# Block-sparse attention and a mixture of experts on one core: three wide token units instead of two, a small tile behind each, and hand order to the last jump

## The chip, the core and the metric

The kernel runs on one core of one Trainium2 chip. A core has five engines that run side by side: TensorE (PE in the profile; its weight loads are PEld), VectorE (DVE), ScalarE (ACT), GpSimd (POOL) and SyncE (SP), and 16 DMA engines that move data between the device's memory and the on-chip memory. Each engine works through its own queue of instructions in order and waits on semaphores for the others. The metric is the device time of one execution in microseconds, the median of several runs.

## The reference

Two blocks stand one behind the other. Attention has 4 batches, 8 heads, 768 tokens and head size 64; a query block of 32 tokens sees its neighbours, the first and last block, and three sampled blocks. Its output is laid out as 3072 rows of 512, and these rows go to eight experts, each row to the one with the largest logit:

```python
logits = x @ w_gate
expert_idx = np.argmax(logits, axis=1)
...
for e in range(E):
    lo, hi = (boundaries[e], boundaries[e + 1])
    ...
    h = np.maximum(x_sorted[lo:hi] @ w1[e], 0.0)
    y_sorted[lo:hi] = h @ w2[e]
y = y_sorted[inv_perm]
return (gate_w[:, None] * y).astype(np.float32)
```

Everything is float32. One expert has two matrices, w1 of 512 x 1024 and w2 of 1024 x 512, 2 MB each. How many rows an expert gets is known only at run time.

## The kernel before

**Attention** goes over 16 pairs of heads, four for each batch. For each pair and half of the queries it computes scores, their exponentials, the weighted values and the division, and writes rows of x to a scratch tensor in memory (`x_rows`). It fills the first half of the time and is not touched by the change.

**Routing** runs beside it. `ranks`, `count` and `layout_a` (phase A) place what is known after three batches: the first KA = 5 tiles of 128 rows, all of one expert each. Phase B (`layout_b`, lines 568 to 653) places the rest after the last batch. It turns counts into four kinds of work on VectorE, with vectors of eight numbers, one per expert:

- a *tile*: 128 rows of one expert (`turn_x`, `layer1`, `layer2`);
- a *unit*: more than 128 rows of one expert in one go, so that a remainder does not need a tile of its own (`gather_u`, `turn_u`, `layers_u`, `leave_u`). In layer 1 and layer 2 the weights stand still and the rows stream past, `width` of them, and four transposes per 128 rows put the result back into rows. The width is one of a few, chosen at run time by a `Switch` on `kind` (line 1036);
- a *small tile*: at most 32 rows of one expert, four column groups of TensorE at once (`gather_s`, `turn_s`, `layer1_s`, `turn_h`, `layer2_s`, `leave_s`);
- *tiles that may not come*: the program has NS tile places in its main loop. If routing needs more, a last `Switch` on `arm` (line 1067) runs 1, 2, ... further tiles; arm 0 runs none. `judge` (line 375) computes the arm, and also sends the whole kernel to a careful second pass if a check on the sums fails.

An expert's remainder behind its last full tile becomes part of a unit if it is at most QR rows and the expert has a tile to join it with; remainders of at most QS = 32 rows that stand alone become small tiles. NS (line 58) is the number of tile places that the worst allowed split needs once the units and small tiles are taken out.

**The main loop** (lines 996 to 1064) is a pipeline written out in program order. In step i it gathers the rows of tile i+3 (an indirect DMA that GpSimd issues), computes layer 1 of tile i+1, between its two halves turns the rows of tile i+2 (16 transposes of 32 x 32 blocks on VectorE), and computes layer 2 of tile i, which ScalarE scales by the gate weight and GpSimd scatters to `out`. Before step AT[u] unit u stands between layer 2 of tile AT[u]-1 and layer 2 of tile AT[u]. In step AT_S[k] small tile k is woven into layer 1 of tile i+1. A unit's rows are gathered in step AT[u]-3 and turned in step AT[u]-2.

**Weights** are fetched by SyncE, 2 MB at a time, into two buffers for w1 and two for w2, in the order of `in_order` (line 737): `fetch_after(what, layer)` fetches what stands two places behind `what`, since that one's buffer has just come free. A fetch waits for the last matmul that read the buffer. SyncE issues in its own queue's order.

**Who sets the order.** `tc.manual_schedule` (the stack `by_hand`) keeps TensorE, VectorE and GpSimd in program order. It is closed after step KA+1 = 6; from there on a scheduler orders all engines. ScalarE and SyncE are ordered by the scheduler throughout.

**On-chip memory.** Units and small tiles use slices of `ea`, the attention's large buffer: `hT_u`, `zT_u`, `xT_u`, `xg_u`, `zo_u` and, behind them, `xg_s`, `xT_s`, `hT_s`.

Of the kernel before, what the change touches and what calls it, by code (L numbers as in the profile page):

```python
# [7 lines left out]
F32 = mybir.dt.float32  # L8
BF16 = mybir.dt.bfloat16
I32 = mybir.dt.int32  # L10
AX = mybir.AxisListType.X
AF = mybir.ActivationFunctionType
ALU = mybir.AluOpType
# [4 lines left out]
def kernel(  # L18
# [11 lines left out]
    nc = tc.nc  # L30
    P = 128
# [7 lines left out]
    N, DM = out.shape  # L39
    E = moe_w_gate.shape[1]  # L40
    F = moe_w1.shape[2]
    DB = DM // P
    FB = F // P
# [2 lines left out]
    TA = NT - NCH  # L46
    KA = 5

    QR = P // 2
    MW = P + QR  # L50
    AT = (10, 13)
    KU = len(AT)

    QS = P // 4
    AT_S = (10, 13, 17)
    KS = len(AT_S)
    NS = KA - -(N - KA * P - KU * MW - KS * QS) // P
    NTB = NC - KA
    NB_ = NTB + 2 * KU + KS
    assert KA < AT[0] - 4 and AT[0] + 3 <= AT[1] < NS - 3 and AT_S[:KU] == AT and AT_S[-1] < NS - 3  # L60
    assert TA * P - E * (P - 1) > (KA - 1) * P
    XW = DM + 8
    scale = 1.0 / float(D) ** 0.5
# [131 lines left out]
    by_hand = ExitStack()  # L195
# [5 lines left out]
    sm = ctx.enter_context(tc.tile_pool(name="sm", bufs=1))  # L201
# [23 lines left out]
    rt = {}  # L225
# [268 lines left out]
    def small_e(name):  # L494
        return sm.tile([P, E], F32, name=name)
# [72 lines left out]
    def layout_b():  # L568
# [9 lines left out]
        nt, up, last = small_e("ntB"), small_e("upB"), small_e("last")  # L578
# [25 lines left out]
        w, ws, to = small_e("w"), small_e("ws"), small_e("to")  # L604
# [18 lines left out]
        )  # L623
        rt["more"] = more_f

        kind = small_e("kind")
        nc.vector.tensor_single_scalar(kind[:], last[:], QR / 2.0, op=ALU.is_gt)
        nc.vector.scalar_tensor_tensor(kind[:], in0=kind[:], scalar=1.0, in1=u[:], op0=ALU.add, op1=ALU.mult)

        xf = sm.tile([1, 2 * KU + KS], F32, name="xfU")  # L630
        for j, (number, n_, what) in enumerate(((at, KU, rt["eid"]), (at, KU, kind), (ws, KS, rt["eid"]))):
# [3 lines left out]
                op=ALU.is_equal,  # L635
# [94 lines left out]
    def gather(i):  # L730
        xg = st[i]["xg"] = keep_xg[i % 4]
        nc.gpsimd.indirect_dma_start(  # L732
            out=xg[:], out_offset=None, in_=x_d[: N - S, :] if i < KA else x_d[:, :], in_offset=bass.IndirectOffsetOnAxis(ap=of("g", i, P), axis=0),
        )
# [34 lines left out]
    def fetch_after(what, layer):  # L769

        fetch_at(orders[layer].index(what) + 2, layer)
# [49 lines left out]
    def layer2(i, group):  # L821
        zp = upper["ps_z"].tile([P, DM], F32, name="zp")
        layer2_pe(i, zp)
        zo = xp.tile([P, DM], F32, name="zo")
        weigh(i, zo, zp)
        put(of("s", i, P), zo[:], group)
# [9 lines left out]


    flat = ea.rearrange("p a b -> p (a b)")
    sizes = (FB * MW, DB * MW, DB * MW, 2 * XW, 2 * DM)
    parts = [flat[:, sum(sizes[:j]) : sum(sizes[: j + 1])] for j in range(len(sizes))]  # L840
    rest = flat[:, sum(sizes) :]
    hT_u = parts[0].rearrange("p (f t) -> p f t", f=FB)
    zT_u, xT_u = (p_.rearrange("p (c t) -> p c t", c=DB) for p_ in parts[1:3])
    xg_u, zo_u = (p_.rearrange("p (j w) -> p j w", j=2) for p_ in parts[3:])

    xg_s, xT_s, hT_s = (rest[:, a:b] for a, b in ((0, XW), (XW, XW + P), (XW + P, XW + 3 * P)))
    h_s, zo_s = parts[0][:, : 2 * P], parts[0][:, 2 * P : 3 * P]
    out_s = out.rearrange("n (g d) -> (n g) d", g=4)
    assert DB == 4 and F == 4 * 2 * P

# [40 lines left out]
    def leave_s(k_, group):  # L891
        put(rt["sS"][:, k_ : k_ + 1], zo_s, group, out_s)
# [102 lines left out]
    index = {}  # L995
    for i in range(NS):
        if i == 0:
            ranks("B", TA, NT)
        gather(i + 3)
        here = AT_S.index(i) if i in AT_S else None  # L1000
        if here is not None:
            layer1_s(here)
            fetch_after(("small", here), 1)
        if i + 1 < NS:
            layer1(i + 1, lambda: turn_x(i + 2), *([turn_h] if here is not None else []))
            if i + 3 <= NS:
                fetch_after(i + 1, 1)
        if here is not None:
            layer2_s(here)
            fetch_after(("small", here), 2)  # L1010
            leave_s(here, "rows_out")
        if i == 0:
            count("B")
            layout_b()
        if i + 3 in AT:
            gather_u(AT.index(i + 3))
        if i + 3 in AT_S:
            gather_s(AT_S.index(i + 3))
        if i + 2 in AT:
            turn_u()  # L1020
        if i + 2 in AT_S:
            turn_s()
        if i in AT:

            continue
        if i + 1 in AT:


            u = AT.index(i + 1)
            zps = [upper["ps_z"].tile([P, DM], F32, name="zp") for _ in range(2)]  # L1030
            zos = [xp.tile([P, DM], F32, name="zo") for _ in range(2)]
            banks = [upper["ps_h"].tile([P, DM], F32, name="hpu", tag="hp") for _ in range(2)]
            banks += [upper["ps_m"].tile([P, DM], F32, name="tpu", tag="tpg") for _ in range(2)] + zps[1:]
            layer2_pe(i, zps[0])
            fetch_after(i, 2)
            for more in tc.Switch(index[u], 3):
                weigh(i, zos[0], zps[0])
                layers_u(u, P + more * QR // 2, banks)
                layer2_pe(i + 1, banks[1])
                weigh(i + 1, zos[1], banks[1])  # L1040
            fetch_after(("unit", u), 1)
            fetch_after(("unit", u), 2)
            fetch_after(i + 1, 2)
            put(of("s", i, P), zos[0][:], "rows_out")
            leave_u(u, "rows_out")
            put(of("s", i + 1, P), zos[1][:], "rows_out")
            continue
        layer2(i, "rows_out")
        if i + 2 <= NS:
            fetch_after(i, 2)  # L1050
        if i == 1:
            tokens("B", NT, NB_)
        if i == 2:
            judge()
            tokens_s()
        if i == 3:
            for u in range(KU):
                at = rt["xeU"][0:1, KU + u : KU + u + 1]
                index[u] = {
                    mybir.EngineType.PE: nc.tensor.value_load(at, min_val=0, max_val=2),  # L1060
                    mybir.EngineType.Activation: nc.scalar.value_load(at, min_val=0, max_val=2),
                }
        if i == KA + 1:
            by_hand.close()
    lent.close()

    for arm in tc.Switch(nc.values_load(rt["arm"][0:1, 0:1], min_val=0, max_val=REDO), REDO + 1):
        inside = ExitStack()
        if arm < REDO:
            lend(inside, ps_h=2, ps_m=2, ps_z=2)  # L1070
            last = NS + arm
            if arm > 1:
                for layer in (1, 2):
                    fetch(NS + 1, layer)
            for i in range(NS, last):
                if i + 3 < last:
                    gather(i + 3)
                layer1(i, *([lambda: turn_x(i + 1)] if i + 1 < last else []))
                if i + 2 < last:
                    fetch_after(i, 1)  # L1080
                layer2(i, "rows_out")
                if i + 2 < last:
                    fetch_after(i, 2)
        else:
            lend(inside, ps_s=2, ps_t=1)
            attention_again()
            lend(inside, ps_h=2, ps_m=2, ps_z=2)
            ranks("A", 0, TA)
            count("A")
            layout_a()  # L1090
            slots_a()
            for part in range(2):
                one_hots("A", rt["slA"], TA, KA, part)
            tokens("A", TA, KA)
            ranks("B", TA, NT)
            count("B")
            layout_b()
            tokens("B", NT, NB_)
            tokens_s()
            for i in range(NC):  # L1100
                gather(i)
                fetch(i, 1)
                fetch(i, 2)
                turn_x(i)
                layer1(i)
                layer2(i, "rows_again")
            for j in range(KU):
                gather_u(j)
                for layer in (1, 2):
                    fetch(("unit", j), layer)  # L1110
                turn_u()
                layers_u(j, MW, [upper["ps_h"].tile([P, DM], F32, name="hpu", tag="hp") for _ in range(2)] + [upper["ps_m"].tile([P, DM], F32, name="tpu", tag="tpg") for _ in range(2)] + [upper["ps_z"].tile([P, DM], F32, name="zpu", tag="zp")])
                leave_u(j, "rows_again")
            for j in range(KS):
                gather_s(j)
                for layer in (1, 2):
                    fetch(("small", j), layer)
                turn_s()
                layer1_s(j)
                turn_h()  # L1120
                layer2_s(j)
                leave_s(j, "rows_again")
        inside.close()
# [30 lines left out]
```

## Time and profile before

| | |
|---|---|
| time, median of 3 runs | 735.09 us (734.4 to 736.08) |
| span of the profiled run | 732.0 us |
| granted TensorE clock, mean | 0.989 |
| weight transfers (w<-in_moe_w_dram) | 54 of 2048 KB |
| read from HBM | 140.39 MB |
| TensorE busy, 0 to 360 / 360 to 540 / 540 to 700 us | 99% / 98% / 99% |
| DMA busy share, 360 to 540 / 540 to 700 us | 0.85 / 0.99 |

Attention ends at some 355 us; the experts take the rest. A busy TensorE in this profile only means that a matmul was under way; how long a piece of work takes is best read from where one group of matmuls starts and the next one does. "s", "op" and "sp" are attention's tiles, "hp" is layer 1 of a tile, "zp" layer 2, "hpu" and "tpu" a unit's (and, with L814, layer 2 of the tile behind it), "hps", "tps_" and "zps" a small tile's. Waits are named by what ended them.

### The profile page before, as it was taken

Reading aid. Unit: us, or ns where it says so; the run is one execution under the profiler, and the core shown is the slowest. Engines: PE = TensorE matmul, PEld = TensorE weight load, DVE = VectorE, ACT = ScalarE, POOL = GpSimd, SP = SyncE. Lnnn points to the kernel's source line nnn. Section 1 sums busy time; section 2 is a strip of 40 time slices with the busy share of each in tenths; the row PEclk is TensorE's granted clock in tenths of the full one; section 3 lists DMA queues with packets and bytes.
Section 4 is the critical chain, followed back from the end, with each engine's and each line's share of the span. In section 5 each row is a group of like instructions: output and inputs, shape, how many; then the busy total and the mean of one; then the engine's idle time right before and its main releaser. Section 6 shows DMA issues by size and latency. Waiting matters only on the chain.

```text
span 732.0 us, 13123 instructions
## 1 busy us (share of the span) xinstructions
PE 707.4 (97%) x5158; PEld 456.2 (62%) x5158; DVE 399.9 (55%) x835; ACT 280.3 (38%) x452; POOL 75.9 (10%) x116
## 2 busy tenths in 40 slices
PE   8999999999999999999999899999999999999991
PEld 5555555555555555555777666776967786866750
DVE  6678778677777778999566435323124502333300
ACT  3766765766676675575311111111121121111110
POOL 7000000000000000000212111211132012111120
PEclk9999999999999999999999999999999999999996
DMA  8322332331332332291399879999779989999983
GB/s 195 88 59 52 87 87 69 88 79 45 74 88 70 83 87 66 72 388 47 91 302 339 308 282 348 318 344 352 271 282 400 372 308 369 376 396 366 380 285 119
DMA packets 117838, 154.32 MB, mean 211 GB/s; under 512 B 56308, under 2 KB 72756, under 8 KB 117749
## 3 DMA queue, kind: packets, MB, share of 16 engines
q1 hardware_dynamic: 111104, 138.23, 56.6%
q0 software_dynamic: 4512, 14.55, 5.2%
q8 instruction: 49, 0.80, 0.5%
q10 hardware_dynamic: 2132, 0.41, 0.3%
q14 instruction: 41, 0.33, 0.2%
HBM read 140.39 MB, written 12.88 MB: 209 GB/s over the span
## 4 chain that ended last, share of the span: by engine, by line
PE 80%; issue 12%; DMA 2%; DVE 2%; POOL 2%; ACTq 0%; ACT 0%; POOLq 0%
PE s L236 17%; PE op L257 17%; PE hp L800 14%; PE zp L814 10%; PE s L239 4%; PE sp L270 3%; PE xr L290 3%; PE tp L216 2%; PE hpu L814 2%; PE hpu L918 1%; PE tpu L926 1%; PE hpu L926 1%; PE tpu L918 1%; DMA ea<-x_rows,gB 1%; DVE ea L907 1%
## 5 line engine op out<-in xcount | busy, mean ns | idle before, releaser
L800 PEld LDWEIGHTS hp<-xgT,w 128*128 128x128 f32 x1344 | 154.6, 193 | 8.8 <-issue 6.8
L236 PE MATMUL s<-qT,kT 64*128 64x384 f32 x768 | 157.0, 487 | 1.2 <-DVE qT L221 1.2
L800 PE MATMUL hp<-xgT,w 128*128 128x128 f32 x1344 | 156.5, 277 | 0.9 <-ACT hT L807 0.9
L241 ACT ACTIVATE ea<-s 128x768 f32<-128x768 f32 x192 | 152.2, 812 | 6.5 <-PE s L239 4.4
L781 DVE STREAM_TRANSPOSE xgT<-xg 32x128 f32<-32x128 f32 x256 | 77.5, 303 | 128.9 <-PE hp L800 61.5
L814 PE MATMUL zp<-w,hT 128*128 128x512 f32 x304 | 134.0, 593 | 0.4 <-DMA w<-in_moe_w_dram 0.4
L247 DVE TENSOR_TENSOR esum<-esum,ea 128x768 f32<-128x768 f32 x128 | 122.6, 958 | 13.7 <-ACT ea L241 0.5
L257 PE MATMUL op<-ea,v_sb 128*64 128x384 f32 x768 | 129.3, 486 | 0.0
L257 PEld LDWEIGHTS op<-ea,v_sb 128*64 128x64 f32 x768 | 55.1, 137 | 68.8 <-issue 68.3
L814 PEld LDWEIGHTS zp<-w,hT 128*128 128x128 f32 x304 | 56.3, 190 | 65.2 <-issue 65.2
L236 PEld LDWEIGHTS s<-qT,kT 64*128 64x128 f32 x768 | 66.3, 187 | 37.6 <-issue 34.9
L277 DVE RECIPROCAL r<-ss 128x128 f32<-128x128 f32 x96 | 82.2, 912 | 1.3 <-ACT ss L272 1.3
L807 ACT ACTIVATE hT<-hp 128x512 f32<-128x512 f32 x40 | 23.9, 597 | 126.4 <-PE hp L800 114.5
L247 DVE TENSOR_TENSOR esum<-ea 128x768 f32<-128x768 f32 x32 | 30.7, 958 | 59.8 <-ACT ea L241 59.8
L239 PE MATMUL s<-pen,oh 64*128 64x384 bf16 x384 | 62.8, 322 | 0.0
L819 ACT ACTIVATE zo<-zp,xg 128x512 f32<-128x512 f32 x19 | 13.1, 687 | 125.1 <-PE zp L814 118.3
L262 ACT COPY oT<-op 128x384 f32<-128x384 f32 x32 | 15.3, 479 | 106.1 <-PE op L257 106.1
L239 PEld LDWEIGHTS <-oh 64*128 64x128 bf16 x384 | 18.9, 94 | 25.1
L829 POOL DMA_INDIRECT out_dram<-zo,sB x16 | 16.1, 1008 | 171.0 <-ACT zo L819 136.1
L907 DVE STREAM_TRANSPOSE ea<-ea 32x128 f32<-32x128 f32 x48 | 13.8, 296 | 36.7 <-PE hps L868 29.6
L290 PEld LDWEIGHTS xr<-mix,oT 128*64 128x64 f32 (+1 forms) x372 | 24.1, 139 | 10.7 <-issue 10.7
L732 POOL DMA_INDIRECT xg<-x_rows,gA x5 | 6.1, 1225 | 220.6 <-ACT ea L241 219.4
(276 smaller groups left out, 458.0 us busy)
## 6 DMA issues: line engine op xcount, KB each, us to landing
w<-in_moe_w_dram SPq DMA_DIRECT2D x54, 2048.0 KB
k_sb<-in_k_dram SPq DMA_DIRECT2D x32, 192.0 KB
v_sb<-in_v_dram SPq DMA_DIRECT2D x16, 384.0 KB
x_rows<-xb SPq DMA_DIRECT2D x16, 384.0 KB
q_sb<-in_q_dram SPq DMA_DIRECT2D x30, 192.0 KB
sums<-ss SPq DMA_DIRECT2D x32, 3.0 KB
q_sb<-in_q_dram ACTq DMA_DIRECT2D x2, 192.0 KB
xg<-x_rows,gB POOLq DMA_INDIRECT x19, 7.4
```

Of the source, the lines that this page charges most:

```text
L236: nc.tensor.matmul(s[:, hh, :CW], lhsT=kT[r, c * P : (c + 1) * P], rhs=qT[r, cols], start=True, stop=False)
L239: nc.tensor.matmul(s[:, hh, :CW], lhsT=oh[r, c, :], rhs=pen[r, cols], start=False, stop=True)
L241: nc.scalar.activation(e, s[:, :, :CW], AF.Exp, scale=scale)
L247: nc.vector.tensor_add(t[:], es[(n, half, 0)] if c == 1 else t[:], e)
L257: nc.tensor.matmul(op[hh * D : (hh + 1) * D, :], lhsT=v_sb[:, hh, c, :], rhs=e[:, hh, :], start=(c == 0), stop=(c == NCH - 1),)
L270: nc.tensor.matmul(sp[hh * D : (hh + 1) * D, :], lhsT=ones[:], rhs=esum[:, hh, :], start=True, stop=True)
L277: nc.vector.reciprocal(r[:, m * P : (m + 1) * P], ss[:, m * P : (m + 1) * P])
L290: nc.tensor.matmul(xr[j * M_ : (j + 1) * M_, m, :], lhsT=oT[:, m * P + j * M_ : m * P + (j + 1) * M_], rhs=mix[:, pr, :], start=True, stop ...
L781: nc.vector.transpose(xT[d, :, t], xg[t, :DM].rearrange("p (c q) -> p c q", c=DB)[:, :, d])
L800: nc.tensor.matmul(hp[:, m, :], lhsT=st[i]["w1"][:, c, fb * P : (fb + 1) * P], rhs=st[i]["xT"][:, c, :], start=(c == 0), stop=(c == DB - 1),)
L807: nc.scalar.activation(hT[:, g * (FB // 2) : (g + 1) * (FB // 2), :], hp[:], AF.Relu)
L814: nc.tensor.matmul(zp[:], lhsT=st[i]["hT"][:, fb, :], rhs=st[i]["w2"][:, fb, :], start=(fb == 0), stop=(fb == FB - 1),)
```

## The change

It does four things. Units take remainders of up to QR = 96 rows, not 64, in widths of 128 to 224 in steps of 16, not 32; there are three of them, at 8, 11 and 14, not two at 10 and 13. A small tile stands behind each unit; before, the third one stood alone at 17. TensorE, VectorE and GpSimd keep program order up to the last jump, so layer 2 of the tile behind a small tile is written out there, and the loop passes over it in its next step. And gathers for tiles that may not come are fewer: tile NS+2 is gathered only in the arms that run it. Besides, `tokens_s` moves from step 2 to step 4, away from `judge`, and `zo_u` moves into the space of `hT_u`, since the wider units need more of `ea`.

With these, NS falls from 21 to 18: more rows fit into units, so fewer tile places are written out, and what does not fit is left to the arms.

```diff
-    QR = P // 2
+    QR = 3 * P // 4
+    STEP = P // 8
     MW = P + QR
-    AT = (10, 13)
+    AT = (8, 11, 14)
...
-    AT_S = (10, 13, 17)
+    AT_S = (8, 11, 14)
...
-        kind = small_e("kind")
-        nc.vector.tensor_single_scalar(kind[:], last[:], QR / 2.0, op=ALU.is_gt)
-        nc.vector.scalar_tensor_tensor(kind[:], in0=kind[:], scalar=1.0, in1=u[:], op0=ALU.add, op1=ALU.mult)
+        kind, wide_ = small_e("kind"), sm.tile([1, QR // STEP, E], F32, name="wide_")
+        nc.vector.tensor_scalar_mul(kind[:1, :], last[:1, :], 1.0 / STEP)
+        nc.vector.tensor_tensor(
+            wide_[:], kind[0:1, None, :].to_broadcast([1, QR // STEP, E]),
+            rt["kx"][0:1, : QR // STEP].unsqueeze(2).to_broadcast([1, QR // STEP, E]), op=ALU.is_gt,
+        )
+        nc.vector.reduce_sum(kind[:1, :], wide_.rearrange("p k e -> p e k"), axis=AX)
+        nc.vector.tensor_tensor(kind[:1, :], kind[:1, :], u[:1, :], op=ALU.mult)
...
-    sizes = (FB * MW, DB * MW, DB * MW, 2 * XW, 2 * DM)
+    sizes = (FB * MW, DB * MW, DB * MW, 2 * XW)
...
-        gather(i + 3)
+        if i + 3 <= NS + 1:
+            gather(i + 3)
...
             layer2_s(here)
             fetch_after(("small", here), 2)
+
+            layer2(i + 1, "rows_out")
+            fetch_after(i + 1, 2)
             leave_s(here, "rows_out")
...
-        if i in AT:
+        if i in AT or i - 1 in AT:
             continue
...
-            for more in tc.Switch(index[u], 3):
+            for more in tc.Switch(index[u], QR // STEP + 1):
                 weigh(i, zos[0], zps[0])
-                layers_u(u, P + more * QR // 2, banks)
+                layers_u(u, P + more * STEP, banks)
...
             judge()
+        if i == 4:
             tokens_s()
...
-        if i == KA + 1:
-            by_hand.close()
+    by_hand.close()
     lent.close()
...
+            if arm > 2:
+                gather(NS + 2)
```

More of the change, by code (lines that the diff above doesn't have):

```diff
@@ L59 @@
     NB_ = NTB + 2 * KU + KS
-    assert KA < AT[0] - 4 and AT[0] + 3 <= AT[1] < NS - 3 and AT_S[:KU] == AT and AT_S[-1] < NS - 3
+    assert KA < AT[0] - 2 and all(b - a > 2 for a, b in zip(AT, AT[1:])) and AT_S == AT and AT[-1] < NS - 3
     assert TA * P - E * (P - 1) > (KA - 1) * P
@@ L843 @@
     zT_u, xT_u = (p_.rearrange("p (c t) -> p c t", c=DB) for p_ in parts[1:3])
-    xg_u, zo_u = (p_.rearrange("p (j w) -> p j w", j=2) for p_ in parts[3:])
+    xg_u, zo_u = (p_.rearrange("p (j w) -> p j w", j=2) for p_ in (parts[3], parts[0][:, : 2 * DM]))
     xg_s, xT_s, hT_s = (rest[:, a:b] for a, b in ((0, XW), (XW, XW + P), (XW + P, XW + 3 * P)))
-    h_s, zo_s = parts[0][:, : 2 * P], parts[0][:, 2 * P : 3 * P]
+    h_s, zo_s = (parts[0][:, 2 * DM + a * P : 2 * DM + b * P] for a, b in ((0, 2), (2, 3)))
     out_s = out.rearrange("n (g d) -> (n g) d", g=4)
@@ L1059 @@
                 index[u] = {
-                    mybir.EngineType.PE: nc.tensor.value_load(at, min_val=0, max_val=2),
-                    mybir.EngineType.Activation: nc.scalar.value_load(at, min_val=0, max_val=2),
-                }
-        if i == KA + 1:
-            by_hand.close()
+                    mybir.EngineType.PE: nc.tensor.value_load(at, min_val=0, max_val=QR // STEP),
+                    mybir.EngineType.Activation: nc.scalar.value_load(at, min_val=0, max_val=QR // STEP),
+                }
+    by_hand.close()
     lent.close()
```

## The prediction

> **What bounds the kernel.** I read the summed busy times first, then the 40 slices, then TensorE's timeline over the expert stage with GpSimd and SyncE beside it, and last the waits. From the page, parts 1 and 2:
>
> ```profile
> PE 707.4 (97%) x5158; PEld 456.2 (62%) x5158; DVE 399.9 (55%) x835; ACT 280.3 (38%) x452; POOL 75.9 (10%) x116
> ...
> PE   8999999999999999999999899999999999999991
> ...
> DMA  8322332331332332291399879999779989999983
> ```
>
> TensorE is busy from end to end, and in the last third the DMA engines are nearly full too: from 540 to 700 us their busy share is 0.99. In the DMA packets I cut the weight traffic into 2 MB pieces: 26 transfers, landing from 551.1 to 709.2, run back to back, 6.35 us each. So TensorE sets the end, and the weights are just in time behind it. TensorE's timeline (start, duration, operation):
>
> ```profile
> 505.78 7.03 PE L814 MATMUL zp<-w,hT 128*128 128x512 f32 x16
> 512.65 5.36 PE L918 MATMUL hpu<-ea,w 128*128 128x192 f32 x32
> ...
> 534.52 7.03 PE L814 MATMUL hpu<-w,hT 128*128 128x512 f32 x16
> 541.48 1.93 PE L868 MATMUL hps<-w,ea 128*32 128x256 f32 x32
> ...
> 581.65 4.51 PE L918 MATMUL hpu<-ea,w 128*128 128x160 f32 x32
> ...
> 600.08 7.03 PE L814 MATMUL hpu<-w,hT 128*128 128x512 f32 x16
> ```
>
> Starts give the prices. A plain tile recurs every 14.02 us (layer 2 is 6.87 of it, layer 1 7.15). A unit of 192 tokens takes 512.65 to 534.52, 21.87; one of 160 takes 581.65 to 600.08, 18.43; so 32 tokens cost 3.44. A small tile woven into its neighbour's layer 1 costs 4.9 (541.48 to 560.49 is 19.01, less 14.02 and 0.1). The third, which stands alone at 661.32, costs 5.67. There is one real hole, in the timeline at 404 to 418 us:
>
> ```profile
> 404.73 7.20 DVE L907 STREAM_TRANSPOSE ea<-ea 32x128 f32<-32x128 f32 x24 [6.61 <-DMA ea<-x_rows,gB]
> 408.85 0.30 PE L389 MATMUL okp<-ones,okn 64*1 64x1 f32 x4
> ...
> 411.96 0.15 DVE L391 TENSOR_SCALAR bad<-okp 1x1 f32<-1x1 f32 x1
> ...
> 412.17 0.55 PE L707 MATMUL tps<-tvB,fourfold 128*128 128x3 f32 x2 [3.02 <-DVE bad L391]
> ...
> 412.58 5.28 PE L800 MATMUL hp<-xgT,w 128*128 128x128 f32 x32
> ```
>
> The scheduler put the first unit's 24 transposes ahead of `bad`; `tps` shares `okp`'s bank and waits 3.02 us. The next half layer takes 5.11 us to the next start instead of 3.65. Layer 2 follows at 421.70 where 409.15 + 7.66 = 416.8 was possible: 4.9 us lost.
>
> **What the Trainium skill says.** "TensorE: Matmul & The Clock Gate", section "What's actually happening": the array falls to half clock after an idle window of some 3.4 us and needs as long to recover. The trace agrees: the granted clock averages 0.91 at 400 to 420 and the half layer after the hole is slow. "DMA: Bandwidth & Descriptors", section "Issuing engines are not separate DMA queues": transfers from all queues run on the same 16 engines. Agreed: weight transfers last 5.2 to 6.1 us alone and 7 to 8 when row gathers and scatters run beside them. "Runtime: NRT & Kernel Launch", section "Instruction fetch mechanics": a taken branch outside the fetched pages waits for a DMA. Agreed: TensorE's compare-and-branch took 4.95 us before the first unit and 6.12 before the second. It hid behind the 6.87 us of layer 2 already queued.
>
> **The change, part by part.** Routing the input by the reference's arithmetic gives 431, 32, 256, 32, 256, 160, 593, 1312 tokens per expert; the five first tiles take 256 of expert 0 and 128 each of experts 4, 5 and 6. Before: units for expert 0 (remainder 47, width 192) and expert 7 (remainder 32, width 160), as the trace shows; three small tiles; 16 tiles left, 21 with the five, which is NS. After, a remainder of 81 (expert 6) is a unit too: width 128 + 6 x 16 = 224. Expert 0's becomes 176, expert 7's stays 160. 14 tiles are left, 19 with the five, and NS is 18: one tile runs in arm 1 of the last jump. So two tiles fewer, one unit more.
>
> - Two tiles: 2 x 14.02 = -28.0.
> - Unit of 224: 21.87 + 3.44 = 25.3, with 0.1 at its exit. No row has this width; from below, 224/192 x 21.87 = 25.5 agrees. +25.4.
> - Expert 0's unit at 176: half of 3.44, -1.7.
> - Third small tile, woven in: 4.9 - 5.67 = -0.8.
> - The hole: in program order `bad` comes right after `okp`, and `tps` two tiles later finds its bank free. -4.9, and 0.4 for `tps` itself: -4.5.
> - Slot planning: two more VectorE operations and wider ones, some 0.5 (rows of 0.15 to 0.2 each). TensorE already waits for the one-hots at 393.46, so this shows: +0.5.
> - The 0.43 wait for the last weights (709.73) goes: four fewer transfers (50, not 54), and the last but one tile's weights land before the final jump.
> - Arm 1: TensorE reads the arm at 709.80, as soon as the last layer 2 is queued, and its branch to the neighbouring arm took 0.31; the layer 2 of tile 17 hides it. ScalarE's branch (0.4 to 4.4) has 3.6 us of layer 1 before the first relu is asked for and 7.1 before layer 2 needs it. +0.3. The tail from the end of TensorE to the end of the span, 716.84 to 732.0, stays 15.2, since scatter and final drain are the same.
> - Fewer gathers, zo_u inside hT_u, prefetched spare weights: no engine waits for them; hidden behind the final layers. 0.
>
> Sum without new waits: -28.0 + 25.4 - 1.7 - 0.8 - 4.5 + 0.5 - 0.4 + 0.3 = -9.2.
>
> **New waits.** By hand order, the second and third units' gathers are queued on GpSimd behind two scatters that wait for the next tile's layer 2; before, they went out at 538.49 and 539.78, under the unit. Count from the start S of the small tile. Layer 2 ends at S+18.9, its scaling 0.9 later; five GpSimd issues 1.3 apart put the second gather at S+24.0. Gathers took 5.9 to 8.7 to land, so S+30 to S+32.7. Then 28 transposes at 0.3 (96 tokens, not 64) on VectorE, which queues nothing else that is urgent: xT_u is ready at S+38.4 to S+41.2. TensorE asks for it at S + 19.0 + 21.1 = S+40.1. Wait: 0 to 1.1 per unit, twice.
> SyncE's order now has the unit's w2 ahead of its w1. Before, w1 landed at 575.1 for a use at 581.65, 6.5 early; one 5.3 us transfer ahead of it, and 1.9 more of gathers moved into this stretch, make it 0.7 late. Bounds -1 and 3.3 by the spread of transfer times. The branch has 0.5 us of slack before it shows. These overlap at one point, so I take 1.0 for each of two units: +2.0. Total -7.2: 735.1 - 7.2 = 727.9.
>
> **Rivals.** (1) All waits vanish: -9.2, 725.9. For it: gathers at 6 us, w1 one microsecond earlier. (2) The weights become the bound: w1 is 3.3 late at both units, and such a hole costs 1.5 more in clock, as at 412.58: -9.2 + 9.6, 735.5, no change. For it: DMA share 0.99, five fetch pairs per 65 to 72 us where a pair needs 12.7. Against: that is 63.5. (3) Hand order hurts: gathers behind scatters, transposes and fetches late together, 5 us and the clock at each unit, 1 us at the first: -9.2 + 14, 739.9, slower. For it: GpSimd and VectorE now wait strictly in line. Against: I followed the queue around each unit and found only the 1.1 above.
>
> **Chances.** Forecast (726.5 to 731) 0.58; rival 1 0.2; rival 2 0.13; rival 3 0.09. The first two are faster, and a third of rival 2 is: 0.82 faster, 0.05 the same, 0.13 slower. The range: the lower end is rival 1 with a faster tail by a microsecond or so, 724.3; the upper takes in most of rival 2, 733.5.
>
> **What would show it.** The plan: unit rows of 176, 224 and 160, 50 weight transfers, layer 1 in the last arm. The hole: `tps` without a wait. The new waits: idle TensorE before the second and third unit, put down to the transposes or to the weights. Wrong if a unit starts more than 3 us late, if TensorE idles in the last arm, or if an arm other than 1 runs.

## The result and the profile after

The changed kernel takes 723.31 us (median of 4 runs, 722.53 to 724.0); the kernel before, beside it, 734.75. The ratio is 0.9849, with an interval of 0.9818 to 0.9879. The prediction was 727.9 with a range from 724.3: right in direction, 4.6 us too slow, and the time lies one microsecond below the range.

The traces that follow are of one execution each: 733.71 us before, a microsecond faster than the median, and 724.0 after, the slowest of its four. So the medians differ by 11.4 us and the two traces by 9.7.

The page of the changed kernel, parts 1 and 2:

```profile
PE 701.8 (97%) x5134; PEld 457.6 (63%) x5134; DVE 393.6 (54%) x825; ACT 281.2 (39%) x456; POOL 72.6 (10%) x114
...
PE   8999999999999999999999999999999999899993
...
DMA  9312323322333322193278899996999399979950
```

TensorE is still busy nearly everywhere, for 5.6 us less, and the span fell by 9.7, from 732.0 to 722.3. That difference says that part of the time was won where TensorE does not work. The timeline of TensorE in the changed kernel (start, duration, operation; the wait ahead of it in brackets), first where the hole was (`okp` is the matmul of `judge`, `tps` that of `tokens_s`), then around the three units:

```profile
409.20 0.30 PE L390 MATMUL okp<-ones,okn 64*1 64x1 f32 x4
409.43 3.84 PE L806 MATMUL hp<-xgT,w 128*128 128x128 f32 x32
...
417.12 3.17 PE L820 MATMUL zp<-w,hT 128*128 128x512 f32 x7
...
438.00 0.28 PE L713 MATMUL tps<-tvB,fourfold 128*128 128x3 f32 x2
...
480.26 4.94 PE L924 MATMUL hpu<-ea,w 128*128 128x176 f32 x32
...
500.52 7.03 PE L820 MATMUL hpu<-w,hT 128*128 128x512 f32 x16
...
540.78 7.03 PE L820 MATMUL zp<-w,hT 128*128 128x512 f32 x16
549.47 6.29 PE L924 MATMUL hpu<-ea,w 128*128 128x224 f32 x32 [1.65 <-DMA w<-in_moe_w_dram]
...
574.96 7.03 PE L820 MATMUL hpu<-w,hT 128*128 128x512 f32 x16
...
615.23 7.03 PE L820 MATMUL zp<-w,hT 128*128 128x512 f32 x16
624.51 4.58 PE L924 MATMUL hpu<-ea,w 128*128 128x160 f32 x32 [2.25 <-DMA w<-in_moe_w_dram]
...
643.12 7.03 PE L820 MATMUL hpu<-w,hT 128*128 128x512 f32 x16
```

Between `okp` and the next layer 2 there is no hole any more (7.92 us instead of 12.85), and `tps` comes two tiles later without a wait. The first unit follows its layer 2 at once. The second and third do not: counted from the usual 6.87 us from the start of a layer 2 to what follows it (its pitch) they start 1.82 and 2.41 us late, and the bracket names a weight transfer.

The end of both kernels in the timeline: TensorE's last row, the scaling and the last scatter. Before:

```profile
709.73 7.11 PE L814 MATMUL zp<-w,hT 128*128 128x512 f32 x16 [0.43 <-DMA w<-in_moe_w_dram]
716.92 0.69 ACT L819 ACTIVATE zo<-zp,xg 128x512 f32<-128x512 f32 x1 [6.85 <-PEq L1067]
717.88 1.00 POOL L829 DMA_INDIRECT out_dram<-zo,sB  x1 [5.24 <-ACT zo L819]
```

After:

```profile
704.27 7.03 PE L820 MATMUL zp<-w,hT 128*128 128x512 f32 x16
711.39 0.69 ACT L825 ACTIVATE zo<-zp,xg 128x512 f32<-128x512 f32 x1 [6.32 <-PE zp L820]
712.35 0.98 POOL L835 DMA_INDIRECT out_dram<-zo,sB  x1 [13.01 <-ACT zo L825]
```

The last scatter is the last thing that counts as work in both. From its issue to the end of the span it is 14.1 us before and 9.9 after. TensorE ends at 716.84 and at 711.30, and what comes behind that is called the tail. Cut at the same four places, the two spans compare like this:

| stretch | before | after | difference | predicted |
|---|---|---|---|---|
| start to `okp` | 408.85 | 409.20 | +0.35 | +0.5 |
| `okp` to the layer 2 after it | 12.85 | 7.92 | -4.93 | -4.9 |
| from there to the end of TensorE | 295.14 | 294.18 | -0.96 | -2.8 |
| end of TensorE to end of span | 15.16 | 11.00 | -4.16 | 0 |
| span | 732.0 | 722.3 | -9.7 | -7.2 |

So two things were to be explained: a tail that shrank although its work was the same, and units that wait longer than forecast.

### The profile page after: what moved, and what is told of

The parts are those of the page before. It is cut to its first block, busy times and chain, and to the rows that moved or that the text cites. A ratio compares the mean times of both kernels' runs of the same rounds, so it can differ in the third digit from the quotient of the medians.

```text
span 722.3 us, 13053 instructions
## 1 busy us (share of the span) xinstructions
PE 701.8 (97%) x5134; PEld 457.6 (63%) x5134; DVE 393.6 (54%) x825; ACT 281.2 (39%) x456; POOL 72.6 (10%) x114
## 4 chain that ended last, share of the span: by engine, by line
PE 57%; issue 33%; POOL 4%; DVE 3%; DMA 1%; POOLq 0%; ACTq 0%; another core or an unknown queue 0%; DVEq 0%
PE s L237 17%; PE op L258 17%; PE hp L806 6%; PE s L240 4%; PE sp L271 4%; PE xr L291 3%; PE zp L820 3%; PE tp L217 2%; POOL out_dram L835 2%; POOL xg L738 1%; DMA q_sb<-in_q_dram 1%; DVE orB L668 0%; POOL ea L858 0%; POOL ea L903 0%; DVE tkB L688 0%
## 5 line engine op out<-in xcount | busy, mean ns | idle before, releaser
L806 PEld LDWEIGHTS hp<-xgT,w 128*128 128x128 f32 x1216 | 138.3, 192 | 7.8 <-issue 5.1
L806 PE MATMUL hp<-xgT,w 128*128 128x128 f32 x1216 | 140.7, 276 | 1.4 <-ACT hT L813 1.4
L787 DVE STREAM_TRANSPOSE xgT<-xg 32x128 f32<-32x128 f32 x208 | 62.9, 302 | 128.6 <-PE hp L806 98.8
L820 PE MATMUL zp<-w,hT 128*128 128x512 f32 x256 | 112.7, 594 | 0.0
L820 PEld LDWEIGHTS zp<-w,hT 128*128 128x128 f32 x256 | 47.5, 190 | 54.6 <-issue 54.6
L813 ACT ACTIVATE hT<-hp 128x512 f32<-128x512 f32 x36 | 21.5, 597 | 114.3 <-PE hp L806 106.4
L825 ACT ACTIVATE zo<-zp,xg 128x512 f32<-128x512 f32 x16 | 11.0, 687 | 101.7 <-PE zp L820 101.7
L913 DVE STREAM_TRANSPOSE ea<-ea 32x128 f32<-32x128 f32 x84 | 21.7, 285 | 29.7 <-DMA ea<-x_rows,gB 29.0
L291 PEld LDWEIGHTS xr<-mix,oT 128*64 128x64 f32 (+1 forms) x372 | 24.1, 139 | 10.7 <-issue 10.7
L835 POOL DMA_INDIRECT out_dram<-zo,sB x14 | 14.0, 1004 | 167.2 <-ACT zo L825 119.1
```

The costliest lines, as they stand in the source:

```text
L291: nc.tensor.matmul(xr[j * M_ : (j + 1) * M_, m, :], lhsT=oT[:, m * P + j * M_ : m * P + (j + 1) * M_], rhs=mix[:, pr, :], start=True, stop ...
L787: nc.vector.transpose(xT[d, :, t], xg[t, :DM].rearrange("p (c q) -> p c q", c=DB)[:, :, d])
L806: nc.tensor.matmul(hp[:, m, :], lhsT=st[i]["w1"][:, c, fb * P : (fb + 1) * P], rhs=st[i]["xT"][:, c, :], start=(c == 0), stop=(c == DB - 1),)
L820: nc.tensor.matmul(zp[:], lhsT=st[i]["hT"][:, fb, :], rhs=st[i]["w2"][:, fb, :], start=(fb == 0), stop=(fb == FB - 1),)
L835: ins = nc.gpsimd.indirect_dma_start(out=to[:, :], out_offset=bass.IndirectOffsetOnAxis(ap=at, axis=0), in_=rows, in_offset=None, bounds_c ...
```

## Experiments

Times are medians, ratios are to the kernel before, run beside each. The stretch from `okp` to the end of TensorE, read from each trace, is given beside the time, since the time to `okp` differs by up to 3 us between executions (408.5 to 411.5) of code that is alike up to there.

**Which arm runs.** The instruction records of GpSimd's queue show what the page leaves out (start, duration, what it is):

```
before (arm 0)                               after (arm 1)
717.88  1.00  last scatter                   712.29  0.04  semaphore wait
719.17  2.83  semaphore wait                 712.35  0.98  last scatter
722.13  1.38  INC_SWDGE_SEM                  712.37  1.32  INC_SWDGE_SEM
723.54        branch                         713.73        branch
726.18  4.97  DRAIN                          716.63  4.81  DRAIN
```

Before, GpSimd waits for the landing of the scatter, which comes at 721.97; after, it doesn't. The first theory was that arm 0 costs this wait. One more tile place in the changed kernel makes arm 0 run, with all else alike:

```diff
-    NS = KA - -(N - KA * P - KU * MW - KS * QS) // P
+    NS = KA - -(N - KA * P - KU * MW - KS * QS) // P + 1
```

> The changed kernel with one more tile place in the main loop (NS 19, not 18), so the 19th tile is computed in the loop and the last jump takes arm 0; nothing else differs. Theory A (the 4.1 us that the tail lost, 15.2 to 11.1 us from the end of TensorE to the end of the span, come from the last scatter: in an arm that holds the scatter itself GpSimd does not wait for its landing before its final drain, in arm 0 it does): TensorE ends where it did, at 711 within 1 us, the tail is 15 us again, the time 723.3 + 4 = 727.4. Rival B (the tail is short because fewer weights are in flight, or because a landing happened to be quick): the tail stays at 11 to 12, the time 723 to 724.

Measured: 729.45 us (728.16 to 732.9), ratio 0.9942 (0.9926 to 0.9958). The median is 2 us above the expectation; the profiled execution, at 728.16, is the fastest. In its trace TensorE takes 302.5 us from `okp` to its end (302.1 in the changed kernel) and the tail is 15.0, not 11.0. GpSimd waits 2.60 us for the scatter, from 713.85 on. The tail goes with the arm.

**Spare weights.** For arm 0 two weight transfers are made that nobody will use, the last landing at 720.7 in the kernel before. They could be what the end waits for:

```diff
-            if i + 3 <= NS:
+            if i + 3 < NS:
                 fetch_after(i + 1, 1)
...
-        if i + 2 <= NS:
+        if i + 2 < NS:
             fetch_after(i, 2)
...
-            if arm > 1:
+            for n_ in range(min(arm, 2)):
                 for layer in (1, 2):
-                    fetch(NS + 1, layer)
+                    fetch(NS + n_, layer)
```

> As the kernel with NS 19, but the weights of the tile that does not come are not fetched ahead (48 + 2 transfers instead of 52); an arm that needs them would fetch them itself. Theory A: tail still 15 us, time as with NS 19. Rival C (in arm 0 the spare weights, still on their way, are what SyncE and the end wait for): tail back at 11 us, 4 us faster than with NS 19.

Measured, on top of the diff of the last run: 729.72 us (one time), a tail of 14.2, and GpSimd again waits for the scatter (issued at 714.79, landed at 718.2). Without the spare weights the tail is within a microsecond of what it was with them. They are not it.

**The same in the kernel before.** One tile place fewer there, so that its last tile runs in arm 1:

```diff
-    NS = KA - -(N - KA * P - KU * MW - KS * QS) // P
+    NS = KA - -(N - KA * P - KU * MW - KS * QS) // P - 1
...
-    assert KA < AT[0] - 4 and AT[0] + 3 <= AT[1] < NS - 3 and AT_S[:KU] == AT and AT_S[-1] < NS - 3
+    assert KA < AT[0] - 4 and AT[0] + 3 <= AT[1] < NS - 3 and AT_S[:KU] == AT and AT_S[-1] <= NS - 3
```

> The kernel before with one tile place fewer in the main loop (NS 20, not 21): its last tile runs in arm 1 of the last jump; two weight transfers fewer. Theory A (a scatter inside an arm lands beside GpSimd's final drain): TensorE ends within 1 us of where it did, the tail shrinks from 15.2 to 11.1 us, time 734.0 - 4 = 730.0. Rival H (the short tail belongs to the changed kernel only): tail 15 us, time 733 to 735.

Measured: 734.72 us (12 runs), ratio 0.9996 (0.998 to 1.0011): nothing. The trace says that both halves happened. The tail is 11.0 us, as the theory has it. But TensorE ends at 721.41 instead of 716.84. TensorE's timeline of this run:

```profile
691.92 15.48 PE L814 MATMUL zp<-w,hT 128*128 128x512 f32 x32 [4.18 <-DMA w<-in_moe_w_dram]
707.24 7.31 PE L800 MATMUL hp<-xgT,w 128*128 128x128 f32 x64
714.38 7.03 PE L814 MATMUL zp<-w,hT 128*128 128x512 f32 x16
```

Layer 2 waits 4.18 us for weights that land at 691.88. In the kernel before they land at 691.74, no earlier, but there the scheduler has put the first 36 matmuls of the last tile's layer 1 in front (its row at 681.11 counts 100, not 64), and layer 2 starts at 692.28 without a wait:

```profile
681.11 11.33 PE L800 MATMUL hp<-xgT,w 128*128 128x128 f32 x100
692.28 7.03 PE L814 MATMUL zp<-w,hT 128*128 128x512 f32 x16
```

A tile in the arm is out of the scheduler's reach, so nothing fills the gap. The two layers 2 after the gap then take 15.32 us to the next start, where the changed kernel takes 13.73 (683.39 to 697.12), and the stretches of the trace show why (columns: window, length, busy time of the engines, then granted clock, DMA share, GB/s):

```profile
688.00:692.00 4.00, 0.08 (x1) 0.08 (x1) 0.00 (x0) 0.37 (x1) 0.00 (x0) 0.94 1.01 379
692.00:707.00 15.00, 15.00 (x32) 6.75 (x33) 0.00 (x0) 0.69 (x1) 1.99 (x2) 0.90 0.45 152
```

The clock after the gap averages 0.90. That agrees with the Trainium skill, "TensorE: Matmul & The Clock Gate", section "What's actually happening": the array goes to half clock after an idle window of some 3.4 us. In the kernel before, a hole of 3.02 us was already enough. The win of the tail was real and was given back by a wait of the same size.

**Only the place of one scatter.** What differs between the arms for GpSimd is where the last scatter stands: ahead of the jump in arm 0, inside it in arm 1. So arm 0 runs again, as in the first experiment, and only that scatter moves:

```diff
-        layer2(i, "rows_out")
+        if i == NS - 1:
+            zp_last = upper["ps_z"].tile([P, DM], F32, name="zp")
+            layer2_pe(i, zp_last)
+            zo_last = xp.tile([P, DM], F32, name="zo")
+            weigh(i, zo_last, zp_last)
+        else:
+            layer2(i, "rows_out")
...
         inside = ExitStack()
+        put(of("s", NS - 1, P), zo_last[:], "rows_out")
```

> The changed kernel with NS one higher, so that arm 0 runs (as in the run with arm 0 before), and only the scatter of the last tile moved from ahead of the last jump into its arms; its layer 2 and its scaling stay ahead. Theory A, narrowed (GpSimd, on leaving the jump, waits for the landing of scatters issued ahead of the jump, and not for those issued inside the arm, so it is the place of the last scatter that sets the tail): the tail from the end of TensorE to the end of the span falls from 15.0 to some 11 us, a span of 722.4 and 725.4 us. Rival Q (it is running arm 0 at all that costs, or the jump that comes after the last matmul): the tail stays 15, 729.4 us. Rival R (the scatter waits for GpSimd's own branch inside the arm): GpSimd's branch to arm 0 took some 0.5 us, so at most 0.6 us more than A.

Measured: 725.27 us (723.89 to 726.52), ratio 0.9891 (0.9874 to 0.9908), 4.2 less than the first experiment; the span is 722.2. The end, from TensorE's last four matmuls on:

```profile
708.82 1.88 PE L820 MATMUL zp<-w,hT 128*128 128x512 f32 x4
710.78 0.69 ACT L825 ACTIVATE zo<-zp,xg 128x512 f32<-128x512 f32 x1 [6.23 <-PEq L1083]
711.75 1.00 POOL L835 DMA_INDIRECT out_dram<-zo,sB  x1 [5.90 <-ACT zo L825]
```

TensorE ends at 710.70, so the tail is 11.5. GpSimd's exit waits now come before the scatter and take 0.04 us each; INC_SWDGE_SEM follows at 712.24, the branch at 713.61. So the tail goes with the place of the scatter and not with the arm as such. By the medians this kernel is still 2 us behind the changed one, while the two traces have the same span, 722.2 and 722.3; that difference stays open.

**Which weight comes first.** In the changed kernel the unit's w2 is fetched ahead of its w1, since w2's buffer comes free first. Holding that fetch back until w1's is issued reverses the two for the second and third unit:

```diff
         if i + 1 < NS:
             layer1(i + 1, lambda: turn_x(i + 2), *([turn_h] if here is not None else []))
             if i + 3 <= NS:
                 fetch_after(i + 1, 1)
+            if i - 1 in AT and i + 2 in AT:
+                fetch_after(i, 2)
...
             layer2(i + 1, "rows_out")
-            fetch_after(i + 1, 2)
+            if i + 3 not in AT:
+                fetch_after(i + 1, 2)
```

> The changed kernel with the order of two fetches swapped, for the second and third unit: the unit's w1 before its w2. Theory D (the units start 1.8 and 2.4 us late because w1 stands behind w2 in the DMA queues): w1 lands some 7 us earlier, both units start within 0.3 us of the end of layer 2, TensorE ends 4.2 us earlier, time 723.3 - 4.2 = 719.1. Rival E (the DMA engines as a whole are behind, so that whatever comes second is late): the wait moves to the unit's layer 2 or to the next small tile, time 722 to 724.

Measured: 719.16 us (718.93 to 719.4), ratio 0.9796 (0.978 to 0.9813), which beats both kernels. TensorE's timeline at the two units:

```profile
540.29 7.03 PE L820 MATMUL zp<-w,hT 128*128 128x512 f32 x16
547.16 6.22 PE L924 MATMUL hpu<-ea,w 128*128 128x224 f32 x32
...
612.84 7.03 PE L820 MATMUL zp<-w,hT 128*128 128x512 f32 x16
619.71 4.51 PE L924 MATMUL hpu<-ea,w 128*128 128x160 f32 x32
```

Both units start 6.87 us after the layer 2 ahead of them: no wait. From `okp` to the end of TensorE it is 297.7 us instead of 302.1; the tail is 11.0 as before. The landings of w1, from the 16 semaphore updates of each transfer:

```
                          issued   first of 16   last of 16   unit starts
after, second unit        533.83   546.90        549.34       549.47
after, third unit         608.27   621.55        624.37       624.51
w1 first, second unit     533.34   542.73        544.71       547.16
w1 first, third unit      605.89   614.93        616.54       619.71
```

In the changed kernel TensorE starts 0.13 us after the last of the 16. In the reordered one, w2 of the second unit lands at 550.37, and the unit asks for it at 559.27.

**Rows out of the way.** The other suspect was the gathers and scatters. First, the next unit's two gathers right behind `leave_u`, 24 us earlier (506.0 instead of 530.3 for the second unit):

```diff
-        if i + 3 in AT:
-            gather_u(AT.index(i + 3))
+        if i + 3 == AT[0]:
+            gather_u(0)
...
             leave_u(u, "rows_out")
+            if u + 1 < KU:
+                gather_u(u + 1)
             put(of("s", i + 1, P), zos[1][:], "rows_out")
```

> The changed kernel with the next unit's two gathers issued right behind the unit's scatters, as the scheduler had them in the kernel before; the order of fetches is left as it is (w2 ahead of w1). Theory I (the two gathers, in the same stretch as the unit's weights, make w1 late): the waits of 1.8 and 2.4 us ahead of the second and third unit shrink to under 0.6 us each, time 723.3 - 3.5 = 719.8. Theory D alone (the place of w1 in the queue is what counts): waits of 1.3 to 2.4 us stay, time 722.5 to 723.3.

Measured: 724.31 us (722.64 to 724.74), not separable from the changed kernel. In the trace the waits of the two units are 1.58 and 1.23, 2.8 in sum instead of 4.2, and `okp` to the end of TensorE is 300.9 instead of 302.1. So moving the gathers takes away a third of the wait, not all of it. Then, on top of that, the small tile's scatter and the next small tile's gather earlier as well, ahead of layer 2 of the tile behind it:

```diff
+            leave_s(here, "rows_out")
+            if i + 3 in AT_S:
+                gather_s(AT_S.index(i + 3))
             layer2(i + 1, "rows_out")
             fetch_after(i + 1, 2)
-            leave_s(here, "rows_out")
...
-        if i + 3 in AT_S:
-            gather_s(AT_S.index(i + 3))
+        if i + 3 == AT_S[0]:
+            gather_s(0)
```

> The changed kernel with the row transfers around a small tile spread out: the next unit's two gathers go out right behind leave_u, and the small tile's scatter and the next small tile's gather go out ahead of layer 2 of the tile behind it. So GpSimd issues three row transfers, not seven, in the 9 us before and while w1 of the second and third units is on its way; the fetch order of the weights stays as changed. Theory N (the faster version with the scheduler from step 7 on is faster because this crowd of row transfers is gone, and the crowd delays w1 by 1 to 2 us): waits before the two units fall from 4.2 to 1.4 in sum, 723.3 - 2.8 + 0.3 = 720.8. Theory O (the rows move the same bytes through the same 16 engines earlier or later, and w1 is late because w2 stands ahead of it): waits stay at some 4, 722.8 to 723.8.

Measured: 722.21 us (721.86 to 723.99), ratio 0.9844 (0.9823 to 0.9865), by time not separable from the changed kernel either. The waits, in TensorE's timeline:

```profile
549.04 6.29 PE L924 MATMUL hpu<-ea,w 128*128 128x224 f32 x32 [1.18 <-DMA w<-in_moe_w_dram]
...
623.15 4.58 PE L924 MATMUL hpu<-ea,w 128*128 128x160 f32 x32 [1.31 <-DMA w<-in_moe_w_dram]
```

Against the pitch of 6.87 they are 1.34 and 1.48: again 2.8 in sum, the same as with the unit's gathers alone. Three row transfers instead of seven in this stretch, and two thirds of the wait are still there. Neither theory of the pair holds whole: the row transfers count, but for less than the place of w1 behind w2.

**The scheduler from step 7 on**, as before the change, with all else as changed:

```diff
-    by_hand.close()
+        if i == KA + 1:
+            by_hand.close()
```

> The changed kernel with hand order closed after step 6 again, as before; the scheduler orders the rest. It then puts the next unit's gathers right behind the unit's scatters and one tile's transposes into the middle of the unit's. Theory J (hand order from step 7 on is worth nothing by itself, the gathers go early instead): waits ahead of the units as in the run with early gathers, time 720 to 723. Rival K (hand order is what keeps the units on time): a unit starts over 3 us late, time above 726.

Measured: 721.18 us (719.49 to 722.3), ratio 0.98 (0.9769 to 0.983). The units wait 0.96 and 0.39 us, each starting 0.1 us after its w1 is complete, and `okp` to the end of TensorE is 298.9. The fetch order is unchanged, w2 ahead of w1, but w1 is complete 7.7 and 7.1 us after the start of the layer 2 ahead of its unit, instead of 8.6 and 9.1. The scheduler, too, issues the unit's gathers, the small tile's scatter and the next small tile's gather early, which by the run with the rows out of the way is worth half of the 2.9 us by which the waits shrink. Where the other half comes from stays open. Hand order to the last jump thus cost 2 us by the medians (the two intervals just overlap) and 3.2 by the traces, as long as w2 stood ahead of w1.

**What took the hole away.** The change moved `tokens_s` from step 2 to step 4 and also extended the hand order; each could do it. In the kernel before, `tokens_s` alone in step 4:

```diff
         if i == 2:
             judge()
+        if i == 4:
             tokens_s()
```

> The kernel before with tokens_s moved from step 2 to step 4, nothing else. Theory F (the hole at 409 us is tps waiting for the bank that okp holds until bad, which stands behind 24 transposes): tps finds its bank free, the hole and the slow half layer vanish, TensorE ends 4.5 us earlier, time 734.8 - 4.5 = 730.3. Rival G (the hole is paid back by weights that are no earlier): w2 of the next tiles or a later unit waits, time 733 to 735.

Measured: 730.6 us (729.19 to 732.51), ratio 0.9946 (0.9926 to 0.9965). TensorE's timeline of this run:

```profile
410.06 0.30 PE L389 MATMUL okp<-ones,okn 64*1 64x1 f32 x4
410.30 3.84 PE L800 MATMUL hp<-xgT,w 128*128 128x128 f32 x32
...
417.98 7.03 PE L814 MATMUL zp<-w,hT 128*128 128x512 f32 x16
...
454.80 7.38 PE L800 MATMUL hp<-xgT,w 128*128 128x128 f32 x64 [1.54 <-issue]
...
708.98 7.11 PE L814 MATMUL zp<-w,hT 128*128 128x512 f32 x16 [1.85 <-SPq L1068]
```

From `okp` to layer 2 it is 7.92 us, so the hole is gone. The scheduler gave some of it back: at 454.80 layer 1 waits, because VectorE now does the first small tile's transposes at 447.83, for which it waits for their gather, ahead of a relu and of the 16 transposes that this layer 1 needs; and the last layer 2 waits 1.85 us instead of 0.43. In sum it is 306.0 us from `okp` to the end of TensorE instead of 308.0. So theory F is right about the hole and not about the sum: of the 4.5 us by which TensorE was to end earlier the trace has 2.0, and that the median came so close to 730.3 is in part luck.

The other way round, the changed kernel with `tokens_s` back in step 2:

```diff
         if i == 2:
             judge()
-        if i == 4:
             tokens_s()
```

> The changed kernel with tokens_s back in step 2, behind judge, under hand order. Theory L (the hole was made by the transposes that stood ahead of bad, and hand order alone removes it): bad follows okp within 0.4 us, tps waits 0.3 to 0.5 us, layer 1 behind it runs at full clock; the time is that of the changed kernel within a microsecond. Rival M (the shared bank makes the hole, moving tokens_s removes it): tps waits 2 us or more and the next half layer is slow, 4 us longer.

Measured: 722.92 us (one time), 301.7 from `okp` to the end of TensorE. With `tps` right behind `okp` (409.23) it waits 0.2 us, and layer 2 follows `okp` after 8.46 us instead of 7.92. Hand order alone removes the hole but for 0.5 us, as moving `tokens_s` alone removed it in the kernel before: either is enough. With both, nothing is gained in the sum, 302.1 against 301.7. In this run TensorE loses 0.7 to 0.8 us in layer 1 ahead of each of the last two units and then waits only 0.48 and 0.72 for w1, so it reaches late weights later; why layer 1 waits here was not found out.

## Why the prediction was right and wrong

**The failed step** is the sentence that the tail "stays 15.2, since scatter and final drain are the same". The instructions are the same, their order on GpSimd is not. A scatter's entry in the profile lasts 1.0 us, which is the time to issue it. The Trainium skill says so in "Perfetto Trace Analysis", section "DMA Instruction — SWDGE (GPSIMD)": the profiler's end is the end of descriptor generation, not of the data movement. Here the landing came at 721.97, 4.1 us after the issue at 717.88. In arm 0 GpSimd waits for that landing and only then goes on to its closing 8 to 9 us (branch and drain, up to the end of the span). In arm 1 it asks only for the earlier scatters and goes on at once; the one wait for scatters that is left is SyncE's, from 713.87 to 715.29, and it lies beside GpSimd's closing. From scatter to branch it is 5.66 us before and 1.38 after: -4.28, and the drain chain is 0.1 longer. Of the 4.28, 2.83 is the wait itself; most of the rest is GpSimd's own jump, which comes after the scatter in arm 0 and ahead of it in arm 1. The run with the scatter moved into arm 0 shows the effect by itself, with 3.6 us of tail. Of the twelve traces, the four with the last scatter ahead of the jump have tails of 14.2 to 15.2 us, the eight with it inside 10.7 to 11.5. The prediction with this term added is 727.9 - 4.2 = 723.7. That this is nearly the measured time is luck: the next term pulls the other way by 2.2, which gives 725.9, and the traces put the whole change at -9.7 us where the two corrections make -9.2. What is left between 725.9 and 723.31 is mostly the spread between executions that the section on the result names.

**The mis-sized term** is the wait ahead of the second and third unit: +2.0 forecast for the transposes and w1 together, 4.2 measured, all of it for w1. The mechanism, w1 behind w2 in SyncE's order, was right, and reversing the two takes it all away. The size failed at "w1 landed at 575.1". That came from cutting the packets into pieces of 2 MB. The 16 updates of that transfer lie between 574.95 and 577.0, so it was complete 1.9 us later. With 577.0 the prediction's own sum is 5.3 + 1.9 - 4.65 = 2.6 late for each unit; 1.8 and 2.4 came. The closeness is again in part luck, since the 1.9 for gathers moved into this stretch measured only 0.7 for each unit in the runs with the rows early. That each transfer counts to 16, one for each DMA engine, and that these finish independently, stands in the Trainium skill, "DMA: Bandwidth & Descriptors", section "Why a DMA increments its semaphore by 16 and not by 1"; the traces agree, mostly with 2 to 3 us between first and last under load.

**Right by its steps.** Routing: units of 176, 224 and 160 rows, 50 weight transfers, arm 1. The unit of 224 takes 25.49 us (25.4 predicted); expert 0's 20.26 instead of 21.87, -1.6 (-1.7); a small tile woven in 5.0 instead of 5.67, -0.7 (-0.8). The hole: -4.9, from the reason given, with `tps` costing 0.2 later (0.4). Slot planning +0.35 (+0.5), less than the executions differ by. The wait for the last weights went, and arm 1 cost nothing (+0.3). The branch ahead of each unit, suspected to have only 0.5 us of slack, is hidden: with w1 in time the units follow at the pitch. With the measured sizes, the terms of the stretch up to the end of TensorE sum to -0.8 us, and the table has -0.96. So little is left for the two parts that were not run by themselves, the gathers that are not issued and the new place of `zo_u`. Two readings were off without any effect: the 26 transfers are 6.32 us apart, not 6.35, and the longest branch of ScalarE before was 6.3 us, not 4.4 (575.17 to 581.49).

**Too cautious.** `turn_u` did not bite. The transposes end at 544.85 and 619.67, 37.4 and 37.8 us after the small tile's start, where 38.4 to 41.2 was forecast and 40.1 was wanted. The second gather landed in the forecast window; the transposes took 0.27 us each, not 0.3, and the first one ran while the second gather was still coming.

**The rivals.** The waits did not vanish (the first), and the weights did not become the bound (the second), though w1 was late at both units, as it said: by 2.1 us on average and not by 3.3. Hand order does hurt (the third), but by 2 to 3 us and not by 14: 2.9 of the 3.2 us are in the waits ahead of the units, where w2 stands ahead of w1. At the hole it helps by 4.4 if `tokens_s` stays in step 2. The lower end of the range allowed "a faster tail by a microsecond or so"; it was four.

## What to carry to other kernels

Ask of the last scatter which engine waits for its landing, and what that engine still has to do afterwards: placed inside the last runtime jump instead of ahead of it, the landing runs beside the closing work, which was worth 3.6 to 4.2 us of tail here. Fetch in the order of need, not in the order in which buffers come free, when the transfers run back to back (4.4 us here from `okp` to the end of TensorE), and count a transfer as landed with the last of its 16 engines. And a piece of work moved into a jump's arm can no longer fill a gap ahead of the jump: read which gap it filled before moving it.

## What the runs showed that was not expected

- GpSimd closes the program with INC_SWDGE_SEM (1.32 to 1.38 us), a branch (2.5 to 2.9) and a DRAIN (4.8 to 5.0), one after the other. In every trace here this chain ends 0.8 to 0.9 us before the span does.
- Under back-to-back weight transfers the 16 engines finish the same transfer up to 5.0 us apart in the changed kernel (issued at 473.59: 480.83 to 485.80), and 3.3 in another case (622.29: 632.03 to 635.35); with little queued ahead, 0.9 (563.36: 570.31 to 571.17).
- A gap of 4.18 us on TensorE cost a further 1.6 us in the two layers 2 behind it (15.32 instead of 13.73).
